# A spectral filter and a feed-forward layer on one core: the first batch in halves of d, one of them turned by DMA transposes

## The chip, the cores and the metric

The kernel runs on one core of a Trainium2 chip. Its engines are PE (TensorE, matmuls, with PEld for the loads of stationary operands), DVE (VectorE), ACT (ScalarE), POOL (GpSimd) and SP (SyncE, which here only issues DMAs). DMAs are issued on the queues of SP, ACT and POOL and are carried by 16 DMA engines. The metric is the device time of one execution in microseconds (us); lower is better. The kernel before took 740.85 us, the median of 3 runs (740.0 to 741.22).

## The reference

x is 8 batches x 3008 positions x 256 channels (d), all in float32. Each batch is filtered along its positions in the frequency domain, and each of the 24064 resulting rows goes through a feed-forward layer:

```python
X = np.fft.rfft(x, axis=1)
F = (filt_r + 1j * filt_i)[None, :, :]
y = np.fft.irfft(X * F, n=x.shape[1], axis=1).reshape(B * S, D)
h = y @ w_in                      # 256 -> 2048
g = np.maximum(0.01 * h, h)       # leaky ReLU
out = g @ w_out                   # 2048 -> 256
```

## The kernel before

**The filter.** The 3008 positions are taken as 94 x 32 (N1 x N2). The transform is done as two matmul stages: the first contracts over the 94, the second, with the twiddles in its constants (f2_sb), over the 32. The filter is applied as two elementwise products (with the transform and with its real and imaginary rows swapped, `i` = 0 and 1), and two inverse stages follow. A matmul contracts over the partition axis, so between stage one and two, and again between the two inverse stages, the data must be turned: what lay along the free axis must come to lie along the partitions. The end of the filter is yt, 256 channels in two tiles of 128 partitions (`dt` = 0, 1) by a ring of 6 x 512 positions, in fp16.

**The feed-forward part.** 47 chunks of 512 rows. For each, `moe1` (L520) makes 16 column blocks of h on PE (L528) and ScalarE applies the leaky ReLU (L531); the second product is plain for the first three chunks (`plain`, L689) and after that a seven-product scheme (`products`, L633) whose sums and differences VectorE forms. Chunk 0 needs positions 0 to 511 of batch 0, which come from the first two groups h = 0, 1 of 376 positions, in both dt.

**Batches 1 to 7** are worked on beside the feed-forward part. Their first turn is a DMA transpose on SP's queue (`t1_load`, L274, issued at L277), their second goes through DRAM (L341, L285). When each group is issued is set by a planner: `at(time, f)` puts work into a heap by time, in units of which a chunk has SL = 8; PLANS, REST, READ, MARGIN, AFTER and the other constants of L102 to L126 give the due times. Every engine works in the order in which the program issues.

**Batch 0** comes before anything else can start and is written out by hand, in the string FIRST (L482), as a list of steps that is issued in order before the planner begins:

- `xc`, `blank`: rounding the first x columns (loaded early in float32 on SP, L225) to fp16, and zeroing the spare partitions of x_sb;
- `warm n`: n filler matmuls (L384) into a bank that is not read;
- `s1p`, `s1e`: stage one for some columns n0 into a PSUM bank, and its eviction by ACT (A) or VectorE (D) into big[0];
- `t1 i`: the first turn, a quarter of it each, a VectorE transpose of 32x32 blocks (L399);
- `s2p hf c n i b`: stage two for half hf of d, n of the 24 frequencies from c on; `s2d`: the filter product by VectorE straight from PSUM; `s2a`, `s2m`: a copy by ScalarE, then the product by POOL (L416);
- `sap`, `sae`: the first inverse stage (L436) and its eviction (L439) into big[2];
- `t2 i`: the second turn, a quarter each, by VectorE (L445) into big[0];
- `sbp dt h b`, `sbe`: the last inverse stage (L453) and its eviction into yt (L351). What FIRST leaves out of it is done later by the planner (`late_sb`, L464, at the times REST);
- `x 0`, `x 1`, `w_out`: loads of batch 1's x and of w_out, on POOL's queue.

In the kernel before, `t1` and `t2` turn all 256 channels in four quarters, both halves of d go through the same buffers, and all eight groups h of dt 0 and two of dt 1 are in FIRST.

**Queues at the start.** SP: the first constants (L224), six columns of x in float32 (L225), the other constants (L226). POOL, in this order: the other x columns in three loads (L207), two thirds of f2_sb (L230), the filters of the first half of d (L215, four loads with rows of 256 bytes), the rest of f2_sb (L236), the filters of the second half, the constants of the last inverse stage (L237), w_in (L238, 2 MB in float32). POOL issues these between 1.24 and 18.2 us. Its products, and then batch 1's x in two halves and w_out, follow in its order. Of POOL's loads, each waits at its issue for the one eight before it to land.

**The tail.** `last_three` (L668) stores the last four tiles as they become ready: m4_tile the columns of two tiles (of which the second is cut in 120 and 8 rows), m3_tile those of the other two.

Of the kernel before, what the change touches and what calls it, by code (L numbers as in the profile page):

```python
# [11 lines left out]
P = 128  # L12
FP16 = mybir.dt.float16
FP32 = mybir.dt.float32
# [5 lines left out]
N1, N2 = 94, 32  # L20
# [58 lines left out]
def kernel(  # L79
# [26 lines left out]
    READ = 1.712  # L106
    TURN = 0.889
    TURNED = 2.3
    TURNS = 1.015
    MARGIN = 3.838  # L110
    YD = (0.966, 1.75, 0.753, 0.432, 1.2)
    SUMS_FIRST = (0.018, 2.103, 2.35, 4)
    SUMS = (0.322, 1.569, 2.418, 4)
    REST = (5.339, 14.69, 8.396, 11.015, 24.419, 20.72)
# [3 lines left out]
    AFTER = (0.454, 0.757, 1.245, 2.615, 0.39, 0.731)  # L118
# [3 lines left out]
        (0.01, 0.254, 12.6, 1.065, 4.3, 35.584, 2.78, 8.122, 1.518),  # L122
        (23.983, 0.737, 42.87, 2.58, 7.4, 85.174, 2.85, 2.756, 2.12),
# [98 lines left out]
    EARLY = 6  # L222
# [4 lines left out]
    for n0, nn in ((6, 10), (16, 10), (26, 6)):  # L227
        x_load(0, n0, nn)
# [9 lines left out]
    nc.gpsimd.dma_start(w_in_sb[:], moe_w_in.rearrange("(dt p) c -> p dt c", p=P))  # L238
# [6 lines left out]
    nc.vector.memset(big[2][:].rearrange("p (e n t) -> p e n t", n=Q, t=2)[:, :, NC:Q, :], 0.0)  # L245
# [44 lines left out]
    def paired(t):  # L290
        return t[:].rearrange("p (e n t) -> p n e t", n=Q, t=2)

    def spread(dst, n0, ps, copy, e0=0):
        nn, de = ps.shape[1], ps.shape[2] // 2
        copy(paired(dst)[:, ds(n0, nn), ds(e0, de)], ps.rearrange("p n (e t) -> p n e t", t=2))

    E4 = D // 2 // 4

    def first_t1(i):
        a = big[0][:].bitcast(FP32)[:, ts(i, E4 * Q)].rearrange("p (e n r) -> p e n r", n=Q // 2, r=2)  # L300
        o = big[1][:].bitcast(FP32).rearrange("p (n e r) -> p e n r", n=Q // 2, r=2)
        nc.vector.transpose(o[:, ts(i, E4)], a)
# [84 lines left out]
    def s1p(_, n0, n, b):  # L387
        ps = fill(("s1", n0), b, n, D)
        for j in range(0, n, 2):
            nc.tensor.matmul(ps[:, ds(j, 2), :], fwd1[:N1], x_sb[:N1, ds(n0 + j, 2), :],  # L390
                             start=True, stop=True)

    def s1e(_, n0, n, e):
        spread(big[0], n0, held.pop(("s1", n0)), engine[e])

    def t1(i):
        a = big[0][:].bitcast(FP32)[:, ts(i, E4 * Q)].rearrange("p (e n r) -> p e n r", n=Q // 2, r=2)
        o = big[1][:].bitcast(FP32).rearrange("p (n e r) -> p e n r", n=Q // 2, r=2)
        nc.vector.transpose(o[:, ts(i, E4)], a)  # L399
# [424 lines left out]
```

## Time and profile before

| what | value |
|---|---|
| median of 3 runs | 740.85 us (740.0 to 741.22) |
| the profiled execution | 740.64 us, its span 738.8 us |
| PE busy | 730.5 us, 99% of the span |
| DVE, ACT, POOL busy | 69%, 74%, 23% |
| chain that ended last | PE 93% |
| first feed-forward matmul (L528) | 34.71 us after the span's start |
| end of VectorE's last turn in FIRST | 33.74 us |
| x_sb, w_in, w_out loads from issue to landing (median) | 8.1, 13.1, 14.3 us (480 KB, 1024 KB, 1024 KB) |
| last DMA issue (ACT's queue) | 735.85 us, 0.57 us long |

The span runs from the first to the last instruction; the execution's own time has 1.8 us around it. In the page's table of slices each digit is the busy share of one of 40 slices (18.5 us each) in tenths. A DMA share above 1 means that several records are under way in one DMA engine. In a line of the timeline stand start, length, engine, line, operation, the tiles written and read, shapes, count, and in brackets the idle time before it with what ended it. The rows of L528 on PE give 0.21 us for a matmul of 512 columns in a row with others.

### The profile page before, as it was taken

How to read it: one execution, taken by the hardware profiler on the slowest of the kernel's cores; microseconds unless marked ns; L12 is line 12 of the kernel's file. 1: busy time of each engine (PE TensorE's matmuls, PEld its weight loads, DVE VectorE, ACT ScalarE, POOL GpSimd, SP SyncE). 2: the span in 40 equal slices, each digit the busy share in tenths (PEclk: the TensorE clock that was granted, in tenths of full speed). 3: DMA queues.
4: the chain of work that ended last, by engine and by line, in shares of the span. 5: the costliest groups of instructions: out<-in, count | busy, mean ns of one | idle time of the engine just before them, and what ended most of it. 6: DMA issues, size and time to landing. Idle time of an engine off the chain costs nothing.

```text
span 738.8 us, 19530 instructions
## 1 busy us (share of the span) xinstructions
PE 730.5 (99%) x8129; PEld 521.8 (71%) x8129; DVE 508.7 (69%) x696; ACT 549.3 (74%) x763; POOL 168.0 (23%) x171
## 2 busy tenths in 40 slices
PE   8999999999999999999999999999999999999997
PEld 3666677777777777777777777777767777777776
DVE  7878557776677667676777668666767676465566
ACT  4775787887788778887688777888767777777762
POOL 5605411333221312212132322222031220000000
PEclk9999999999999999999999999999999999999999
DMA  9978778778755595556855477434863433112012
GB/s 203 228 109 171 189 150 170 178 172 167 188 134 126 138 193 143 130 145 126 183 131 137 122 157 169 115 90 110 149 172 95 117 106 94 55 55 66 29 46 71
DMA packets 128617, 98.44 MB, mean 133 GB/s; under 512 B 59296, under 2 KB 107296, under 8 KB 128336
## 3 DMA queue, kind: packets, MB, share of 16 engines
q1 hardware_dynamic: 112905, 79.37, 42.0%
q0 software_dynamic: 15056, 17.50, 15.7%
q8 instruction: 63, 1.03, 0.6%
q10 hardware_dynamic: 567, 0.32, 0.2%
q14 instruction: 26, 0.21, 0.1%
HBM read 45.97 MB, written 35.65 MB: 110 GB/s over the span
## 4 chain that ended last, share of the span: by engine, by line
PE 93%; SPq 2%; DMA 2%; DVE 1%; ACT 1%; POOL 0%; issue 0%; POOLq 0%
PE ph L528 42%; PE pf L601 18%; PE po_ps L601 18%; PE pf L269 2%; PE pf L362 2%; PE pf L315 2%; PE pf L337 2%; PE pf L693 1%; DMA x_sb<-in_x_dram 1%; PE po_ps L693 1%; SPq L277 1%; SPq L587 1%; DMA p_b_g<-p_b_g 1%; PE po_ps L384 0%; PE pf L436 0%; ACT yt L351 0%
## 5 line engine op out<-in xcount | busy, mean ns | idle before, releaser
L531 ACT ACTIVATE gt_c<-ph 128x1024 f16<-128x1024 f32 x376 | 385.4, 1025 | 132.3 <-PE ph L528 125.5
L528 PE MATMUL ph<-yt,w_in_sb 128*128 128x512 f16 x1504 | 447.3, 379 | 0.2 <-ACT yt L351 0.2
L601 PEld LDWEIGHTS <-gt_c 128*128 128x128 f16 x2800 | 201.8, 98 | 97.9 <-issue 1.3
L330 POOL TENSOR_TENSOR y_b_g<-p_b_g,p_b_g 128x512 f16<-128x512 f32 x84 | 118.1, 1407 | 421.1 <-DMA p_b_g<-p_b_g 288.1
L601 PEld LDWEIGHTS <-big 128*128 128x128 f16 x2128 | 151.4, 98 | 65.9
L528 PEld LDWEIGHTS <-w_in_sb 128*128 128x128 f16 x1504 | 117.7, 98 | 4.4 <-DVE yt L351 0.4
L324 DVE TENSOR_TENSOR p_b_g<-pf,fb_sb 128x512 f32<-128x512 f32 x78 | 53.7, 688 | 33.8 <-PE pf L315 20.3
L601 PE MATMUL po_ps<-wt_sb,gt_c 128*128 128x128 f16 x704 | 71.8, 219 | 0.0
L601 PE MATMUL pf<-wt_sb,gt_c 128*128 128x128 f16 x688 | 69.3, 219 | 0.0
L601 PE MATMUL pf<-wt_sb,big 128*128 128x128 f16 x704 | 68.7, 219 | 0.0
L601 PE MATMUL pf<-w_out_sb,gt_c 128*128 128x128 f16 x720 | 68.1, 219 | 0.0
L351 ACT CAST yt<-pf 128x376 f16<-128x376 f32 (+9 forms) x136 | 58.1, 441 | 12.2 <-PE pf L362 8.5
L601 PE MATMUL po_ps<-w_out_sb,gt_c 128*128 128x128 f16 x688 | 65.7, 219 | 0.0
L601 PE MATMUL po_ps<-wt_sb,big 128*128 128x128 f16 x688 | 65.5, 219 | 0.0
L567 DVE TENSOR_TENSOR gt_c<-gt_c 128x2048 f16<-128x2048 f16 x43 | 56.9, 1322 | 1.0
L327 DVE TENSOR_TENSOR p_b_g<-pf,fa_sb 128x512 f32<-128x512 f32 x84 | 57.2, 681 | 0.2
L567 DVE TENSOR_TENSOR big<-gt_c,big 128x2048 f16<-128x2048 f16 (+1 forms) x45 | 56.4, 1254 | 0.0
L567 DVE TENSOR_TENSOR big<-big,gt_c 128x2048 f16<-128x2048 f16 (+1 forms) x45 | 56.3, 1252 | 0.1
L567 DVE TENSOR_TENSOR big<-gt_c 128x2048 f16<-128x2048 f16 (+1 forms) x46 | 56.3, 1224 | 0.0
L339 ACT CAST big<-pf 128x512 f16<-128x512 f32 x84 | 49.0, 584 | 9.3 <-PE pf L337 7.4
L270 ACT CAST big<-pf 128x384 f16<-128x384 f32 x90 | 43.0, 479 | 11.5 <-PE pf L269 8.2
L362 PE MATMUL pf<-i_sb,big 128*128 128x94 f16 x448 | 37.0, 206 | 0.0
(98 smaller groups left out, 644.7 us busy)
## 6 DMA issues: line engine op xcount, KB each, us to landing
p_b_g<-p_b_g SPq DMA_DIRECT2D x156, 128.0 KB
out_dram<-ost_c_h SPq DMA_DIRECT2D x118, 128.0 KB
dz<-big SPq DMA_DIRECT2D x42, 256.0 KB
big<-dz SPq DMA_DIRECT2D x56, 192.0 KB
x_sb<-in_x_dram POOLq DMA_DIRECT2D x40, 192.0 KB, 4.2
x_sb<-in_x_dram POOLq DMA_DIRECT2D x2, 768.0 KB, 9.2
w_in_sb<-in_moe_w_in_dram POOLq DMA_DIRECT2D x1, 1024.0 KB, 13.1
w_out_sb<-in_moe_w_out_dram POOLq DMA_DIRECT2D x1, 1024.0 KB, 14.3
```

Source lines behind the costliest of these rows:

```text
L269: nc.tensor.matmul(ps[:, j, :], x_sb[:, 4 * h + j, ts(dt, P)], fwd1m[:, :NW], start=True, stop=True)
L270: copy(turn_in[:, :, dt, :, ds(4 * h, 4)], ps.rearrange("p n (q k) -> p k q n", q=4))
L324: nc.vector.tensor_tensor(p2[:], ps, fb, AL.mult)
L327: nc.vector.tensor_tensor(p1[:], ps, fa, AL.mult)
L330: ("y", b, g), lambda: nc.gpsimd.tensor_tensor(y1[:], p1[:], p3[:], AL.add)))
L339: nc.scalar.copy(st2[h % 3][:, ds(2 * (g % 2), 2), :], ps)
L351: copy(yt[:, dt, ds(to, 4 * n)].rearrange("p (a c) -> p a c", c=4), v[:, ds(a, n)])
L362: nc.tensor.matmul(ps[:, j, :], z2[h % 3][:, j, ts(dt, P)], i1_sb[:, 4 * h + j, :N1], start=True, stop=True)
L528: nc.tensor.matmul(ph[:, j, :], w_in_sb[:, dt, ts(ct, P)], yt[:, dt, ds(ci * CH % RING, CH)], start=(dt == 0), stop=(dt == NDT - 1))
L531: nc.scalar.activation(gts[ci][:, ds(2 * g, 2), :], ph, AF.Lrelu)
L567: nc.vector.tensor_tensor(*(v[:, ds(c0, n)] for v in (o, i0, i1)), op)
L601: nc.tensor.matmul(of[t], a()[:, c, ts(t, P)], w[:, c, :], start=(c == 0), stop=(c == NCH - 1))
```

## The change

- d is split: half 0 (channels 0 to 127) is turned by VectorE before stage two, now in two quarters (`t1`), half 1 by three DMA transposes of eight frequencies each on SP's queue (`turn1`). For that, stage one of half 1 is computed with x as the stationary operand, 96 columns at a time, so that channels lie on the partitions.
- Before the last inverse stage it is the other way round: half 0 is turned by four DMA transposes of eight columns each (`turn2`), half 1 by VectorE in two quarters (`t2`). Half 0's first inverse stage now has the product as the stationary operand: 48 matmuls of 128 columns in place of 12 of 512.
- The steps of FIRST stand in another order; VectorE evicts three of the groups of `sae`. `sbp` in FIRST covers h = 0 to 3 of dt 0 (and 0, 1 of dt 1); h = 4 to 7 of dt 0 are done later, at the times REST0.
- w_in comes in two pieces, as steps of FIRST on POOL's queue; `x 0` is issued ahead of POOL's first product, the second piece of w_in among the products.
- The early x load has eight columns, the other three loads eight each.
- At the end, m4_tile's first store goes to ACT's queue and its second to SP's, and both of m3_tile's to ACT's.
- Constants of the planner have other values.

```diff
-    READ = 1.712
+    READ = 1.863
...
-    REST = (5.339, 14.69, 8.396, 11.015, 24.419, 20.72)
+    REST = (5.723, 13.479, 13.889, 13.394, 25.953, 17.309)
+    REST0 = (0.946, 2.627, 7.4, 12.566)
...
-    EARLY = 6
+    EARLY = 8
...
-    for n0, nn in ((6, 10), (16, 10), (26, 6)):
+    for n0, nn in ((8, 8), (16, 8), (24, 8)):
...
-    nc.gpsimd.dma_start(w_in_sb[:], moe_w_in.rearrange("(dt p) c -> p dt c", p=P))
...
+    half = [t[:, ts(i, HALF)] for t in big for i in range(2)]
+    in0, in1, mid0, mid1, in2, in3 = half
...
+    def s1p(t, n0, b):
+        if t == 0:
+            ps = fill(("s1", t, n0), b, 4, DH)
+            nc.tensor.matmul(ps, fwd1[:N1], x_sb[:N1, ds(n0, 4), :DH], start=True, stop=True)
+            return
+        ps = fill(("s1", t, n0), b, 4, NW)
+        for j in range(4):
+            nc.tensor.matmul(ps[:, j, :], x_sb[:N1, n0 + j, DH:], fwd1m[:N1, :NW], start=True, stop=True)
...
+    def turn1(c, n):
+        nc.sync.dma_start_transpose(mid1[:, ds(c, n)], in1[:, ds(c, n)].rearrange("p k q n -> p (k q n)"))
+
+    def turn2(h, n):
+        nc.sync.dma_start_transpose(out2[:, ds(h, n)], in2q[:, ds(h, n)].rearrange("p n q k -> p (n q k)"))
...
+    def load_w_in(i):
+        half = moe_w_in.shape[1] // 2
+        nc.gpsimd.dma_start(w_in_sb[:, :, ts(i, half)], moe_w_in.rearrange("(dt p) c -> p dt c", p=P)[:, :, ts(i, half)])
...
     def sap(hf, c, b):
         ps = fill(("sa", hf, c), b, 4, DH)
+        if hf == 0:
+            for j in range(4):
+                for i, m in enumerate((inv2r, inv2i)):
+                    nc.tensor.matmul(ps[:, j, :], prods[0][:, i, c + j, :], m, start=(i == 0), stop=(i == 1))
+            return
...
+            if dt == 0:
+                nc.tensor.matmul(ps[:, j, :], out2[:, n2], i1_sb[:, n2, :N1], start=True, stop=True)
+                continue
...
     FIRST = """
+        blank 2, warm 14, blank 3, s1p 0 8 b2, blank 0, xc 4 4 D, blank 1, s1p 0 4 b4, xc 0 4 A, s1p 0 0 b3,
+        s1p 1 0 b0, s1e 0 4 A, s1p 1 4 b1, s1e 1 0 D, s1e 0 0 A, s1e 1 4 A, s1p 0 20 b4, s1p 1 8 b0, s1e 1 8 A,
+        s1p 0 12 b3, s1e 0 8 D, s1p 1 12 b1, s1p 0 16 b0, s1e 0 12 D, s1e 1 12 A, s1p 1 20 b1, s1p 0 28 b3,
+        w_in 0, s1e 0 16 A, s1p 0 24 b2, s1e 1 20 A, s1e 0 24 A, s1e 0 20 D, s1e 0 28 D, t1 1, s1p 1 16 b1,
+        s1p 1 24 b4, s1p 1 28 b2, warm 6, s1e 1 16 A, t1 0, s2p 0 0 8 0 b3, s1e 1 24 A, s1e 1 28 A,
+        s2p 0 0 8 1 b4, turn1 16 8, turn1 0 8, s2p 0 16 4 1 b1, s2p 0 16 4 0 b0, s2a 0 16 4 0, s2d 0 0 8 0,
+        s2a 0 16 4 1, s2p 0 8 8 0 b3, x 0, s2p 0 20 4 0 b2, s2d 0 0 8 1, s2p 0 20 4 1 b0, s2d 0 8 8 0,
+        s2a 0 20 4 0, s2p 0 8 8 1 b4, s2m 0 16 4 0, s2a 0 20 4 1, sap 0 0 b1, sap 0 4 b2, s2p 1 16 4 0 b0,
+        sae 0 0 A, s2d 0 8 8 1, s2p 1 0 8 0 b3, sap 0 8 b1, sae 0 4 A, s2p 1 0 8 1 b4, s2m 0 20 4 0,
+        s2a 1 16 4 0, s2d 1 0 8 0, turn1 8 8, s2p 1 16 4 1 b0, s2d 1 0 8 1, sae 0 8 A, s2m 0 16 4 1,
+        sap 0 12 b2, sap 0 16 b1, s2m 1 16 4 0, s2a 1 16 4 1, s2m 0 20 4 1, sae 0 12 A, s2p 1 8 8 0 b3,
+        sap 0 20 b2, sae 0 16 D, w_in 1, sae 0 20 A, s2d 1 8 8 0, s2p 1 20 4 0 b0, s2m 1 16 4 1, s2p 1 8 8 1 b4,
+        s2a 1 20 4 0, s2p 1 20 4 1 b1, sap 1 0 b2, s2d 1 8 8 1, sap 1 16 b3, sae 1 0 A, sap 1 4 b0, turn2 0 8,
+        sae 1 4 A, turn2 8 8, sap 1 12 b4, turn2 16 8, sap 1 8 b2, s2m 1 20 4 0, s2d 1 20 4 1, x 1, sae 1 12 A,
+        sae 1 16 D, sap 1 20 b1, turn2 24 8, sbp 0 0 b3, sae 1 8 D, sae 1 20 A, t2 1, sbe 0 0 A, warm 2, t2 0,
+        w_out, sbp 0 1 b3, sbe 0 1 D, sbp 0 2 b0, sbe 0 2 D, sbp 0 3 b2, sbp 1 0 b4, sbp 1 1 b1, sbe 0 3 A,
+        sbe 1 0 D, sbe 1 1 A
     """
...
-            soon(0.02, lambda: (nc.sync, nc.scalar)[t].dma_start(*parts[0]))
+            soon(0.02, lambda: (nc.scalar, nc.sync)[t].dma_start(*parts[0]))
...
-            soon(0.02, lambda: store(ci, 2 + t, low[:, t, 1], P, P, queue=(nc.sync, nc.scalar)[t]))
+            soon(0.02, lambda: store(ci, 2 + t, low[:, t, 1], P, P, queue=nc.scalar))
...
+    for h in range(4, 8):
+        at(REST0[h - 4], lambda h=h: late_sb(0, h, act))
```

## The prediction

> **What bounds the kernel now.** First the page's table of slices, for the engine that is full and for the state of the DMA engines.
>
> ```profile
> PE   8999999999999999999999999999999999999997
> DMA  9978778778755595556855477434863433112012
> ```
>
> PE is full from the second slice to the last but one; the DMA engines are fullest in the first two, 0 to 37 us. So I split PE's time at the first matmul of the feed-forward part (answer on stretches: stretch, length, then busy time and count of PE, PEld, DVE, ACT, POOL, clock, DMA share, GB/s).
>
> ```profile
> 0.00:34.70 34.70, 31.70 (x309) 16.70 (x310) 29.76 (x34) 20.55 (x36) 21.92 (x31) 1.00 1.18 217
> 34.70:46.40 11.70, 11.62 (x112) 6.79 (x112) 8.90 (x15) 9.84 (x14) 1.33 (x2) 1.00 0.97 151
> 46.40:735.16 688.76, 687.19 (x7710) 498.35 (x7709) 470.07 (x648) 518.87 (x715) 144.71 (x138) 1.00 0.55 129
> ```
>
> After 34.7 PE works through a fixed list without a hole worth naming; the change can move the start of that list (T0 = 34.71), its content, or the tail. What sets T0, by the chain in order of time and the timeline:
>
> ```profile
> 2.43 9.88 DMA x_sb<-in_x_dram
> ...
> 27.90 1.22 DVE prod L416
> 29.11 2.29 DVE big L445 x2
> ...
> 31.93 2.74 ACT yt L351 x7
> 34.67 0.04 issue
> 34.71 0.38 PE ph L528
> ```
>
> ```profile
> 14.23 4.62 DVE L399 STREAM_TRANSPOSE big<-big 128x1024 f32<-128x1024 f32 x4
> ...
> 18.40 4.51 POOL L416 TENSOR_TENSOR prod<-spare,fa_sb 128x512 f16<-128x512 f32 x4 [0.25 <-DMA fa_sb<-in_filt_i_dram]
> ...
> 23.42 2.30 POOL L416 TENSOR_TENSOR prod<-spare,fa_sb 128x512 f16<-128x512 f32 x2 [0.50 <-DMA fa_sb<-in_filt_i_dram]
> ...
> 29.03 4.71 DVE L445 STREAM_TRANSPOSE big<-big 128x1024 f32<-128x1024 f32 x4
> ```
>
> The reader is to see two clocks: VectorE (turn, filter products, turn; the last turn ends at 33.74, T0 0.97 later), and POOL's loads, whose filters arrive at 18.3 (first half of d) and 23.3 (second).
>
> What the change adds exists already from batch 1 on, as L277, and its company is on record:
>
> ```profile
> L277 SPq DMA_TRANSPOSE big<-big x42: 1247/1330/2988, 49.0 to 532.9; - x42
> ```
>
> ```profile
> 176.38 1.40 SPq L277 DMA_TRANSPOSE big<-big  x1
> ```
>
> ```profile
> 176.43 0.54 POOL L207 DMA_DIRECT2D x_sb<-in_x_dram  x1
> ```
>
> I counted the trace's packet records. A turn of 128x1024 is 1024 records of 256 B; undisturbed, first records come 1.2 us after issue, all 16 engines are taken for 1.3 us, and it lands 3.2 us after issue (48.96 to 52.14); turns in a row follow 1.3 us apart. The one issued at 176.38 met the load of 176.43 (2048 B records): from 178.6 to 179.4 the load passed 47 records and the turn 41; once the load was out the turn ran at 200 per 0.2 us, and ended at 181.5, 2 us late. Over all 112 steps of 0.2 us after 46 us with both queues busy, POOL's queue passed 1533 records and SP's 1266, whatever their sizes. Likewise the second constants load (128 KB, SP, issued 1.66) landed at 9.9, among the x loads. So the rings take turns record by record, and a 256 B record pays for a large one each time.
>
> **The change, part by part.**
>
> *Removed from VectorE:* two of four turns at each end, 2 x 1.155 = 2.3 us and 2 x 1.18 = 2.35 us. *Added:* three evictions (0.66 each, 2.0 us) and one quarter product (0.68) taken from POOL. The first gain is lost: the last x lands at 12.31 as before (same bytes), the two remaining turns end between 16.4 and 17.2 (ScalarE evicts 0.66 + 0.47 + 0.47 + 0.66 per step before them), but the products need the first filters, at 18.3.
>
> *First turns (3 on SP, issued 15.6 to 16.3):* they run beside the filters' 256 B records. Each needs 1.28 us of all engines, 3.8 us in all; this pushes POOL's ring back by 3.8 us if times add, by 0 if they overlap (the filters' DMA share of 1.8 means two records in flight per engine). I take 1.9: second filters at 25.3. VectorE then runs 25.3 + 2 x 1.22 + 0.66 + 2 x 1.22 + 0.68 + 2 x 0.66 + 2 x 1.18 = 35.2; with 1.0 for the last matmuls and evictions T0 cannot be before 36.2 (34.3 to 38.1).
>
> *Second turns (4 on SP):* they wait for all six evictions of the first half. POOL's order puts a second-half product first, so 25.3 + 2 x 1.16 + 0.6 (two matmuls) + 0.66 = 28.9, first records 30.2 (28.6 to 32). What is in POOL's ring then is the point. Before: constants to 24.1, w_in to 28.6, two halves of x to 36.3, w_out to 41.6, without a gap. After: constants, half w_in, x, half w_in, x, w_out; same bytes, since nothing on POOL waits for a turn. w_in passes 52 records a us, x 25, w_out (512 B) 385. By the end of the second x, 36.3 + 1.9 + 0.3 = 38.5, the first turn has passed at most some 270 records of 1024. Beside w_out the pair makes 263 a us if times add and 385 if they overlap, I take 310: the other 750 take 2.4 us, the second turn 3.3, with 0.5 to land 44.7 (41.7 to 47.7). PE's order needs this second turn ahead of the second half's last matmuls: four groups, evictions, 2.0 us (0.97 for two before). T0 = 46.7 (43.7 to 49.7): +12.0 us (9.0 to 15.0). Turns three and four land by then or soon after; their matmuls come 1.9 us after T0 or later.
>
> [...]
>
> *Cold PE:* PE has little after 31 until the first second turn lands. The row nearest is its only other idle time, before the first fillers: their weight loads come 0.42 us apart up to 5.44, then seven in 1.41. Half speed for 4.2 us costs 2.1 if it happens again and 0 if not; I take 2.0, for that row. [...]
>
> *Work moved behind T0:* four groups of four 94-column matmuls, at 0.17 (the like groups of L269 in the chain): +0.7 us, as PE is full there. Their four evictions (0.47) fit in ScalarE's 1.9 us idle of 11.7.
>
> *POOL and SP queue:* the first x load (0.6 to issue) goes ahead of the products, the w_in half (0.7) among them; POOL's first three products still end by 22.5, ahead of the filters at 25.3, and the rest is earlier than the turns. SP has nothing else to issue before 46. The constants load that now feeds the fourth first-stage step lands up to 0.9 later, 10.7; last x at 12.3 and the filters at 18.3 cover it. First-stage matmuls (16 of 512 columns become 8, and 32 of 96) and the 48 small inverse ones lie under those waits; smaller blanking too.
>
> *Tail:*
>
> ```profile
> 734.30 1.45 ACTq L677 DMA_DIRECT2D out_dram<-ost_c_h  x1
> 735.85 0.57 ACTq L587 DMA_DIRECT2D out_dram<-ost_c_h  x1
> ```
>
> The last store waits 0.7 us behind a 120-row one. Swapped, ACT is free at 735.3, but SP has the 120-row store (1.0 to 1.45) and an 8-row one (0.70): the last issue ends 736.05 to 736.45 against 736.42. I take -0.2 (-0.4 to 0).
>
> *Retuned times* move work inside a stretch where PE is full: 0; the two idle spots of PE there sum to about 2 us (1.2 at one wait for POOL near 536, some 0.7 at 34.7 to 46.4), so -1 to +1.
>
> Sum, against the profiled execution's 740.64: +12.0 + 2.0 + 0.7 - 0.2 = 755.1; the median of the runs is 0.2 above that execution, so 755.3.
>
> **The rivals.**
>
> [...]
>
> 2. *Faster.* VectorE's chain is shorter by 4.65 - 2.68 = 2.0 us. If filters and turns never hold it, T0 = 32.7 and the time is 740.64 - 2.0 + 0.7 - 0.2 - 0.7 (the holes behind T0) = 738.4. It decides only if the first filters are there at 17.2, not 18.3, the second by 23, and the second turns land by 31.5. Against: POOL's ring was full from 2 to 43 us.
>
> 3. *No change.* Turns hidden, filters at 18.3 and 23.3 as now: VectorE ends at 33.3, T0 34.3: 740.64 - 0.4 + 0.7 - 0.2 = 740.7.
>
> **How the numbers follow.** Starved turns 0.74, own range 749 to 762 (749.8 = +9.0, no cold PE; 759 = +15.0 and cold, with 1 us for the holes, and more if the turns overlap badly); rival 1 0.12, rival 2 0.07, rival 3 0.07. Two in ten to be left out: the range takes in most of rival 1, 742 to 762. A difference of 0.2% (1.5 us) is about what a measurement of this kernel can tell from none. Faster: rival 2, 0.07. Same: rival 3 and a little of rival 1, 0.09. Slower: 0.84.
>
> **What the profile after would show.** Right: PE waits of several us before L453 for the second turns, first feed-forward matmul at 44 to 50 and not 34.7, first turns' waits of 1 to 3 us more than 3.2, the second filters later than 23.3, weight loads 0.42 apart behind the wait, PE's list from T0 on about 700 us as now. [...] What would break it most is a POOL ring that runs empty around 27 to 33, because w_in's second half or x is issued later than I read from POOL's order.

## The result and the profile after

The changed kernel took 783.74 us, the median of 5 runs (781.45 to 786.58); before took 740.85 (5 runs beside it, 740.0 to 741.57): a ratio of 1.058, with an interval of 1.0548 to 1.0613. The prediction was 755.3 us with a range of 742 to 762: slower, as forecast, but by 42.9 us and not by 14.5. The profiled execution is the fastest of the five, 781.45 us, its span 779.7; the figures below account for it, and not for the 2.3 us between it and the median.

First the page's table of slices after the change (each digit the busy share of one of 40 slices of 19.5 us, PEclk the granted clock in tenths), and the chain by lines:

```profile
PE   7237999999999999999999999999999999999997
PEclk7658999999999999999999999999999999999999
DMA  9999577778696559555685549534574432212112
GB/s 204 147 56 169 93 148 180 158 172 182 151 184 156 134 129 189 142 136 145 126 184 131 128 112 166 166 95 114 105 178 124 112 105 82 83 49 68 35 42 69
PE 87%; DMA 8%; SPq 2%; POOL 1%; DVE 1%; ACT 0%; issue 0%; POOLq 0%; DVEq 0%
PE ph L555 40%; PE pf L628 17%; PE po_ps L628 17%; DMA big<-big 6%; PE pf L362 2%; PE pf L337 2%; PE pf L278 2%; PE pf L315 2%; DMA p_b_g<-p_b_g 1%; PE po_ps L720 1%; PE pf L720 1%; DMA x_sb<-in_x_dram 1%; POOL y_b_g L330 1%; SPq L286 1%; PE pf L454 0%
```

PE is now full only from the fifth slice on, where before it was from the second. The telling slice is the third, 39 to 58 us: its DMA digit is 9, and it moved 56 GB/s. The engines of the DMAs were busy and passed almost nothing. The turns (big<-big) are 6% of the chain, 45 us by its pieces below. The same by stretches of the changed kernel, and last the second stretch in the kernel before (length, then busy time and count of PE, PEld, DVE, ACT, POOL, clock, DMA share, GB/s):

```profile
0.00:24.00 24.00, 18.77 (x148) 10.42 (x148) 16.19 (x21) 10.91 (x20) 13.80 (x24) 0.79 1.26 200
24.00:51.00 27.00, 0.61 (x4) 0.34 (x4) 0.00 (x0) 0.58 (x1) 3.67 (x4) 0.53 1.27 95
51.00:58.00 7.00, 6.62 (x96) 6.15 (x98) 3.96 (x4) 2.44 (x5) 1.14 (x1) 0.63 0.69 84
58.00:69.06 11.06, 5.61 (x59) 3.06 (x53) 6.89 (x10) 3.60 (x7) 2.86 (x3) 0.88 1.00 155
69.06:73.20 4.14, 3.91 (x22) 1.91 (x21) 1.46 (x3) 1.91 (x3) 0.54 (x1) 0.50 1.35 183
73.20:775.00 701.80, 698.12 (x7819) 504.82 (x7817) 480.68 (x659) 529.00 (x729) 144.05 (x139) 1.00 0.55 128
```

```profile
24.00:51.00 27.00, 26.35 (x290) 16.26 (x287) 22.28 (x30) 21.49 (x36) 7.55 (x9) 1.00 0.87 158
```

From 24 to 51 us hardly an engine works (PE 0.61 us of 27), and 95 GB/s pass at a DMA share of 1.27; before, the same 27 us moved 158 GB/s at a share of 0.87. After 73.2 PE is full again. The chain in order of time says for what the engines waited:

```profile
16.12 1.36 SPq L409
17.53 33.81 DMA big<-big
...
58.40 0.76 SPq L412
59.20 1.33 SPq L412
60.58 11.35 DMA big<-big
71.97 0.49 PE pf L477 x4
```

and the timeline, on SP and on PE:

```profile
16.12 27.84 SPq L409 DMA_TRANSPOSE big<-big  x3
57.93 4.60 SPq L412 DMA_TRANSPOSE big<-big  x3
```

```profile
67.54 0.81 PE L477 MATMUL pf<-i_sb,big 128*128 128x94 f16 x8 [5.10 <-DMA big<-big]
...
69.06 1.22 PE L555 MATMUL ph<-yt,w_in_sb 128*128 128x512 f16 x2
```

The second of the three first turns, issued at 17.53, landed at 51.3; even to issue three of them took SP 27.84 us. T0 is 69.06 (46.7 was forecast, 34.71 is before's). The sum over the trace closes: T0 +34.35, from T0 to the last matmul 705.81 for 699.91 (+5.9), from there to the span's end 4.79 for 4.21 (+0.6), together 40.8 over before's span of 738.8.

Landings by the semaphores, with what was forecast: first turns 29.4, 51.3, 56.1; second filters 38.2 (25.3); w_in's first half 46.6; x's first half 50.1; second turns issued at 57.9 to 62.6 (28.9) and landed at 61.2, 67.5, 71.9, 76.6. I counted packet records: from 21 to 23.5 us the filters and the turns passed one for one, some 330 a us each; then, with the first 6144-byte records of i1 (the constants of the last inverse stage), the turns' 256-byte records began to last up to 2.4 us (18 ns alone), i1's up to 3.9 (0.24 in the kernel before). Of SP's 2840 records from 20 to 52 us, 631 lasted over 0.15 us. Both streams were held, where the prediction had only the turns wait.

### The profile page after: what moved, and what is told of

It is laid out like the page before. It is cut to its first block, busy times and chain, and to the rows that moved or that the text cites. A ratio compares the mean times of both kernels' runs of the same rounds, so it can differ in the third digit from the quotient of the medians.

```text
span 779.7 us, 19560 instructions
## 1 busy us (share of the span) xinstructions
PE 733.7 (94%) x8134; PEld 526.7 (68%) x8134; DVE 509.5 (65%) x696; ACT 548.4 (70%) x764; POOL 166.1 (21%) x171
## 4 chain that ended last, share of the span: by engine, by line
PE 87%; DMA 8%; SPq 2%; POOL 1%; DVE 1%; ACT 0%; issue 0%; POOLq 0%; DVEq 0%
PE ph L555 40%; PE pf L628 17%; PE po_ps L628 17%; DMA big<-big 6%; PE pf L362 2%; PE pf L337 2%; PE pf L278 2%; PE pf L315 2%; DMA p_b_g<-p_b_g 1%; PE po_ps L720 1%; PE pf L720 1%; DMA x_sb<-in_x_dram 1%; POOL y_b_g L330 1%; SPq L286 1%; PE pf L454 0%
## 5 line engine op out<-in xcount | busy, mean ns | idle before, releaser
L324 DVE TENSOR_TENSOR p_b_g<-pf,fb_sb 128x512 f32<-128x512 f32 x78 | 53.6, 687 | 34.0 <-PE pf L315 21.7
L351 ACT CAST yt<-pf 128x376 f16<-128x376 f32 (+7 forms) x137 | 58.8, 442 | 19.4 <-PE pf L362 9.6
L594 DVE TENSOR_TENSOR big<-gt_c 128x2048 f16<-128x2048 f16 (+1 forms) x46 | 58.9, 1281 | 0.2 <-ACT gt_c L558 0.2
L279 ACT CAST big<-pf 128x384 f16<-128x384 f32 x92 | 44.1, 480 | 12.9 <-PE pf L278 11.1
```

The source lines that it names most:

```text
L279: copy(turn_in[:, :, dt, :, ds(4 * h, 4)], ps.rearrange("p n (q k) -> p k q n", q=4))
L324: nc.vector.tensor_tensor(p2[:], ps, fb, AL.mult)
L351: copy(yt[:, dt, ds(to, 4 * n)].rearrange("p (a c) -> p a c", c=4), v[:, ds(a, n)])
L594: nc.vector.tensor_tensor(*(v[:, ds(c0, n)] for v in (o, i0, i1)), op)
```

## The experiments

Theories: A, the rings of SP and POOL pass record for record and each record takes its own time (the prediction's); B, a large record beside a turn takes many times its own time; C, a backlog of several turns does it; D, in a DMA transpose the 16 DMA engines keep step, and one that is ahead holds its engine, for both queues, until the others come up; D2, D with the order of record sizes that drives the engines apart. Times are of one execution, beside 739.9 to 741.7 of before, where no interval is given.

**Turns and loads alone.** A kernel of its own with turns and loads.

> A kernel that computes nothing of the reference and writes only 128 rows of the output: ten stages, each begun when the one before has landed: three turns of 128x1024 alone; three loads like the constants of the last inverse stage (6144 B records, 128 each) alone, then beside three turns; three x loads (8192 B records) alone, then beside three turns; three small x loads (2048 B) beside three turns; four w_in pieces beside three turns; filter loads (256 B) beside three turns; filters, constants, w_in and x in a row beside three turns; the constants beside one turn. Theory A, the rings alternate record by record and each record takes its own time: three turns alone take 6 us from the first issue to the last landing, three constants loads 6 to 8 us, both together 10 to 12 us; x loads 12 to 14 us, with turns 15 to 18; no stage over 20 us. Theory B, records of several kB beside a turn take many times their own time: the stages with 6144 and 8192 B records take over 25 us with three turns, that with 256 B records 10 to 12 us as under A. Theory C, it is the backlog of several turns: over 25 us with three turns beside any load, but the last stage, with one turn, under 10 us.

The loads began only when the turns had landed, so nothing overlapped. It gives the times alone: a turn lands 3.1 to 3.4 us after its issue, turns in a row are issued some 1.3 us apart, and the 128 records of 6144 bytes of one load begin within 2.8 us.

**Three turns added to before.**

```diff
+    for i in range(3):
+        nc.sync.dma_start_transpose(wt_sb[:, i], f2_sb[:, ts(2, NC // FP), :].rearrange("p k m -> p (k m)"))
```

> The kernel before, with three DMA transposes of 128x1024 added on SP's queue behind the landing of the last third of the second stage's constants (19.2 us); nothing reads what they write before it is overwritten. Theory A: 1500 turn records pass beside filters, constants, w_in and x, POOL's loads come 1.5 to 2.5 us later, first feed-forward matmul at 35 to 37, time 741 to 743. Theory B: constants and w_in are held up as in the changed kernel, 10 us or more; first feed-forward matmul at 45 or later, time 751 or more. Theory C says as B. If the trouble were in how the changed kernel's own steps wait for one another, this kernel would lose nothing: 740 to 741.

767.7 us, 27 more, for three turns that nothing reads. T0 nearly stays (35.84); then PE waits 21.7 us for x:

```profile
PE pf L271 <- DMA x_sb<-in_x_dram: 21.7, 1, 21.7
```

Beside w_in's 4096-byte records (24 to 29 us) both queues passed 48 records a us, one for one and near w_in's own rate (52 in the kernel before), as by A; groups of one number of records on both sides would give the same counts. With the change from w_in to x, at 30 us, both queues nearly stopped, up to 62 (51 GB/s from 30 to 38 us).

**Turns and loads apart.** In the changed kernel POOL issues i1, w_in's first half and x's first half only after the first turns have landed (`hold 1`); then also w_in's second half, x and w_out only after the first two second turns (`hold 2`).

```diff
-    nc.gpsimd.dma_start(i1_sb[:], i1_d.ap())
...
+    def hold(of):
+        t = mid1 if of == 1 else out2
+        nc.gpsimd.tensor_copy(mark[:, 0:1], t[:, 7, 0:1])
+        nc.gpsimd.tensor_copy(mark[:, 1:2], t[:, 15, 0:1])
...
+        ... s2m 0 20 4 1, hold 1, i1, w_in 0, x 0, sae 0 12 A, ...
```

> The changed kernel, but POOL issues the last inverse stage's constants, the first half of w_in and the first half of batch 1's x only after all three first turns have landed (it reads an element of two of them first). The first turns then meet filters alone: all theories have them landed by 28 us, not 56. The second turns still meet w_in and x. Theory A, the prediction's sum for them: first feed-forward matmul at 44 to 52, time 749 to 762. Theory B: the second turns clog as the first did; first feed-forward matmul over 55, time over 763.

> As the run with the first hold, and also the second half of w_in, batch 1's x and w_out are issued only after the first two second turns have landed; so neither set of turns has loads of large records beside it but the end of the constants and the first half of w_in. All theories that blame the loads: first feed-forward matmul at 35 to 41; batch 1's x then comes 5 to 9 us after it and PE waits for it; time 743 to 752. If the turns are slow by themselves in this place, the first feed-forward matmul stays over 50 and the time over 757.

769.22 and 762.75 us. With the first hold the first turns landed at 26.3, 27.7 and 28.5, and the second ones ran as the prediction's rule has it: issued at 33.67 and 35.09 they landed at 51.7 and 56.0, while w_in, x, w_in and x beside them landed some 3 to 4 us apart (39.1, 42.5, 45.4, 49.2), none of them stopped, and w_out at 57.7, in 8.6 us for 5.3 in the kernel before. The waits of PE (line waited for: us in total, times, longest):

```profile
PE ph L486 <- DMA big<-big: 15.0, 1, 15.0
PE pf L421 <- DMA big<-big: 3.1, 1, 3.1
```

So a turn beside large records starves and the loads don't stop: the trace has A's mechanism, though T0 (57.59) and time lie where B was to have them. The expectation had left out that the hold itself puts off the loads, i1 from 16.9 to 29.9 us, and that the turns starve beside them for as much longer. With both holds the second turns land 3 to 6 us after issue and T0 is 41.8, but then PE waits 8.7 us for x, and the time is 11 us over the expected 743 to 752: from T0 to the last matmul it takes 14.5 us more than before, of which the 8.7 are the largest part. Moving the loads away gets T0 and gives it back.

**Loads that run when the turns come.**

> This kernel computes nothing of the reference; it only moves data, in ten stages that wait for each other, and writes 128 rows. In each stage the loads of POOL's queue start first and SP's DMA transposes (128x1024, fp16) come while they run: (1) three turns alone, (2) four loads of constants with 6144-byte records alone, (3) these beside three turns, (4) four x loads with 8192-byte runs alone, (5) these beside three turns, (6) these beside one turn, (7) eight pieces of w_in with 4096-byte records beside three turns, (8) eight filter loads with 512-byte rows beside three turns, (9) two filters, constants, x beside three turns, (10) filter, constants, a piece of w_in and x beside three turns. Theory A (rings alternate record by record and each record takes its own time): no stage takes longer than its loads alone plus 1.3 us a turn, so at most 4 us more; the turns land up to as late as the loads. Theory B (a record of some kilobytes beside a turn takes many times its own time): stages 3, 5 and 7, and 9 and 10, take 15 to 30 us more than their loads alone, stage 8 nothing; stage 6 some third of it. Theory C (only several turns waiting at once do it): stage 6 is as by A, stages 3, 5 and 7 as by B. If no stage stalls, it needs something else than loads and turns together, and the size of records alone is ruled out.

Four x loads took 17.2 us alone, 17.9 beside three turns, 17.8 beside one; four constants 10.4 and 11.3; the turns were starved to the end of them. B falls. Only the last two stages, with small records before large ones, were held, by some 4 us: in the one the last filter load ended on the DMA engines from 162.1 to 166.2, in the other w_in (2048-byte records, before x's 8192) took 6.9 us after the load before it, where a piece takes 2.9.

**One turn at a time, and plain copies.** The three added turns write one tile, so that each waits for the one before; or they are plain copies of the same 256-byte pieces.

```diff
-        nc.sync.dma_start_transpose(wt_sb[:, i], f2_sb[:, ts(2, NC // FP), :].rearrange("p k m -> p (k m)"))
+        nc.sync.dma_start_transpose(wt_sb[:, 0], f2_sb[:, ts(2, NC // FP), :].rearrange("p k m -> p (k m)"))
```

> The kernel before with three DMA transposes at the start that nothing reads, all to one destination, so that each is issued only when the one before it has landed: one turn is under way at any time. With all three issued in a row it took 767.7 us, 27 more than before. Theory C (a backlog of several turns makes the stall): the loads get back most of it, 741 to 750 us, and each turn costs x at most some microseconds. Theory B (any turn beside large records): 755 to 770 us, with x landing at 50 or later. Theory A alone (record by record, each in its own time): 741 to 745 us, since the loads then lose at most 3.8 us.

```diff
+    spread_to = wt_sb[:].rearrange("p i c d -> p (i c d)").rearrange("p (k m) -> p k m", k=NC // FP)
-        nc.sync.dma_start_transpose(wt_sb[:, i], f2_sb[:, ts(2, NC // FP), :].rearrange("p k m -> p (k m)"))
+        nc.sync.dma_start(spread_to[:, :, ts(i, P)], f2_sb[:, ts(2, NC // FP), :])
```

> The kernel before with three plain copies in SBUF at the start that nothing reads, of the same 128x1024 fp16 in the same 256-byte pieces and in the same place on SP's queue as the three DMA transposes that took 767.7 us. If it is the transpose that makes the stall: 740 to 746 us, x landing at 35 to 42 as the ring of the loads is pushed back by no more than the copies' own time (3 x 1.3 us). If any small records on another queue beside the loads of POOL do it: 760 to 770 us, x landing after 50.

751.37 and 741.86 us, beside 739.95 of before. The stretch from 30 to 38 us, first with one transpose at a time, then with copies:

```profile
30.00:38.00 8.00, 5.08 (x89) 3.31 (x87) 4.93 (x6) 4.65 (x12) 0.48 (x1) 0.99 1.83 46
```

```profile
30.00:38.00 8.00, 7.42 (x117) 5.00 (x116) 6.88 (x9) 6.15 (x13) 1.22 (x2) 1.00 1.04 205
```

46 GB/s against 205: it takes a transpose, and one is enough to start a stop, so C falls as its cause; but 751.37 lies between the ranges of C and B, and one turn at a time (the second was issued at 44.6, when x's first half had landed) costs 11 us and three in a row 27. With copies x landed at 34.6 (34.4 before), and of 3120 records on SP none lasted over 76 ns. With the one transpose 201 of 1056 lasted over 150 ns. The 4-byte records at its end show how (26 of them): they began at 34.48, 35.10, 35.74, 36.35, 36.99 and 37.60, 0.62 us apart, which is the time of one x record (0.625), and most lasted from 0.6 up to 6.6 us. Read by theory D, the engines that were ahead waited while another, behind them, passed large record after large record.

**The tail alone.**

```diff
-            soon(0.02, lambda: (nc.sync, nc.scalar)[t].dma_start(*parts[0]))
+            soon(0.02, lambda: (nc.scalar, nc.sync)[t].dma_start(*parts[0]))
...
-            soon(0.02, lambda: store(ci, 2 + t, low[:, t, 1], P, P, queue=(nc.sync, nc.scalar)[t]))
+            soon(0.02, lambda: store(ci, 2 + t, low[:, t, 1], P, P, queue=nc.scalar))
```

> The kernel before with only the tail of the change: the first store of the last four tiles on ACT's queue, the second on SP's, and both of the other pair's on ACT's. By the prediction's step the last issue ends 0 to 0.4 us earlier: 740.65 us, ratio 0.9995 to 1. By the rival read from the trace of the changed kernel, where the last issue ended 0.1 us sooner after VectorE's last addition but the span ended 3.09 us after that issue and not 2.40: 741.2 us, 0.3 to 0.6 us more, too little for the median to tell and to be read from the span behind the last matmul (4.21 us before).

Ratio 0.9999 (0.9989 to 1.0009). From the last matmul to the span's end 4.08 us for 4.21.

**The planner's constants alone.**

```diff
-    READ = 1.712
+    READ = 1.863
...
-    REST = (5.339, 14.69, 8.396, 11.015, 24.419, 20.72)
+    REST = (5.723, 13.479, 13.889, 13.394, 25.953, 17.309)
```

> The kernel before with only the planner's constants of the change (READ, TURNS, MARGIN, YD, SUMS, REST, AFTER, PLANS). The prediction put them at 0, from -1 to +1: 740 to 742 us, ratio 0.999 to 1.001. The changed kernel took 5.9 us more than before from the first feed-forward matmul to the last, of which a cold PE (2.1 us, at half clock from 69.06 to 73.19) and the four late groups (0.7) explain 2.8: if the constants make the other 3.1, this takes 743 to 744 us, ratio 1.003 to 1.005.

742.33 us, ratio 1.0018 (1.0005 to 1.0031), that is 1.3 us (0.4 to 2.3). In its profile T0 to the last matmul takes 701.8 us, 1.9 more than before.

**Turns of the changed kernel as plain copies.** All seven; the three first; the four second ones.

```diff
-        nc.sync.dma_start_transpose(mid1[:, ds(c, n)], in1[:, ds(c, n)].rearrange("p k q n -> p (k q n)"))
+        nc.sync.dma_start(mid1[:, ds(c, n)], in1[:, ds(c, n)].rearrange("p k q n -> p k (q n)"))
...
-        nc.sync.dma_start_transpose(out2[:, ds(h, n)], in2q[:, ds(h, n)].rearrange("p n q k -> p (n q k)"))
+        nc.sync.dma_start(out2[:, ds(h, n)], in2q[:, ds(h, n)].rearrange("p n q k -> p n (q k)"))
```

> The changed kernel with each of its seven DMA transposes of the first batch replaced by a plain copy of the same bytes in the same 256-byte pieces, on the same queue, in the same place (the copies don't turn, so the first batch's result is not the reference's; all other work and all waits are as they were). If the transposes themselves made both streams stop from 24 to 51 us, what is left is the prediction's mechanism, copies passed over record by record: T0 at 44 to 50, 750 to 760 us. If small records on SP's queue beside POOL's loads are enough, 775 to 785 us and T0 near 69.

> The changed kernel with the three first turns alone replaced by plain copies (which don't turn, so half of the first batch's result is not the reference's); the four second turns stay DMA transposes. By the prediction's step for the second turns (starved one record for one, loads at their own rate) T0 is 44 to 50 and the time 750 to 760 us, as with all seven replaced. If the second turns make the loads stop as well where w_in, x and w_out run in sequence beside them: T0 55 to 70, 762 to 785 us.

> The changed kernel with the four second turns alone replaced by plain copies (which don't turn, so half of the first batch's result is not the reference's); the three first turns stay DMA transposes. The changed kernel took 783.74 us, with the first turns as copies 782.95, with all seven as copies 754.19. If each of the two groups makes the loads stop by itself: last first turn at 50 to 57, T0 at 60 to 68, 772 to 782 us. If the first turns' stop was worth nothing (what the second turns cost they cost in any case): 754 to 762 us.

754.19, 782.95 and 780.13 us; T0 42.98, 69.79, 67.59. Either group of transposes stops the loads by itself: with the second as copies the first turns land at 30.7, 53.3 and 59.1; with the first as copies, which land by 24.3, the four second turns bring the stop, and x's second half lands at 68.0. That 754.19 lies so near the forecast is chance. The expectation was wrong on the copies: source and destination were contiguous, and the records were of 2048 bytes, 128 a copy, so they were passed over far less. So once more, each copy split in two of every second block, which keeps pieces of 256 bytes (at twice the DMAs on SP's queue):

```diff
+        for a in range(2):
+            nc.sync.dma_start(mid1[:, ds(c, n)].rearrange("p (k a) m -> p a k m", a=2)[:, a],
+                              in1[:, ds(c, n)].rearrange("p (k a) q n -> p a k (q n)", a=2)[:, a])
```

> The changed kernel with each of its seven DMA transposes replaced by two plain copies of every second block, so that the pieces stay 256 bytes (in the run with seven plain copies whole rows were joined to records of 2048 bytes, 128 a copy; there T0 was 42.98 and the time 754.19). The copies don't turn, so the first batch's result is not the reference's. By the prediction's step for small records passed over one for one: second turns starved beside w_in and x, T0 44 to 50, 750 to 760 us. If small records in that number are enough to stop both queues, transposes or not: T0 over 55, 765 us and more.

769.01 us, T0 58.79. These are the numbers of the second case, but not its cause: no record on SP lasted over 82 ns, and the loads didn't stop. The last filter landed at 27.5 (23.3 before), and from there i1, w_in and x's first half took 11.4 us (11.1 before). But the first turns landed only at 39.5. PE's waits for the turns, before stage two (L426) and before the last inverse stage (L481):

```profile
PE ph L426 <- DMA big<-big: 10.7, 2, 6.7
PE pf L481 <- DMA big<-big: 7.7, 3, 6.3
PE pf L426 <- DMA big<-big: 2.7, 1, 2.7
```

With records passed one for one and nothing held, the change costs 27 us beside the 741.70 of before; with transposes 43.

**What drives the engines apart.** Three kernels that only move data. A load of 20 rows lies on 10 of the 16 DMA engines, two rows on each (six of its 16 updates come 1.5 us after the issue, the ten others at 3.3 us and more, as read in the second of the three), so the others get ahead. The first expectation has its rows spread otherwise, which was wrong.

> Computes nothing of the reference: nine stages that wait for each other, in each some loads on POOL's queue and, while they run, DMA transposes or plain copies of 128x1024 on SP's. Three x loads (96 records of 8192 bytes each, six for each DMA engine) stand alone (stage 1), with two turns (2); behind four small x loads of 20 rows, which give four engines one record more each than the others, so that they fall behind by some 2.5 us (3 alone, 4 with two turns, 5 with two plain copies); behind four x loads of 4 rows (6 alone, 7 with one turn, 8 with one copy); and four loads of constants behind the 20 rows, with two turns (9). Theory D (a turn's records on the 16 engines keep step: an engine that is ahead waits in its turn record for the engine that is behind, and what the loads have on that engine waits too): stages 4, 7 and 9 have turn records of 0.3 us and more, in multiples of the x record's time, and their loads land at least 4 us later than in 3 and 6; stages 5 and 8 have none, with loads at most 2 us later; stage 2 as stage 1 with at most 2 us more. Theory A (record by record, each in its own time): no stage's loads land more than 2 us later for its turns, and no turn record takes over 0.15 us. If 4, 7 and 9 are as 3 and 6, engines out of step are not enough, and what else the kernels bring (engines at work on SBUF, loads of several sizes) stays open.

The small loads wrote one tile and waited for each other, so most turns fell between loads. Two pairs did meet. In one, a turn beside a single load of 20 rows landed 7.95 us after issue and not 3.2, the load 7.4 and not 3.7 to 3.9, with x records of up to 3.9 us; in the other, in the last stage, they took 5.2 and 4.6.

> Computes nothing of the reference: eight stages that wait for each other, each with six loads on POOL's queue, all into tiles of their own: four small ones of x rows of 8192 bytes, then two of 96 such rows. In stages 1 to 4 the small ones have 20 rows (these lie on 10 of the 16 DMA engines, two on each, so that the other six come 5 us sooner to the large loads), in 5 to 7 32 rows (two on every engine); stage 8 has two loads of constants (6144 bytes, 128 rows) in their place. Beside them come, some microseconds later, on SP: nothing (1, 5), one DMA transpose (2), two (3, 6, 8), two plain copies in the same 256-byte pieces (4, 7). Theory D (in a turn the engines keep step; one that is ahead waits in its turn record for one that is behind, and holds the loads' records on it): the last load lands in 2 and 3 at least 4 us later than in 1, with turn records of 0.3 us and more; in 4, 6, 7 and 8 at most 2.6 us later than in 1 or 5, with no turn or copy record over 0.15 us but at the ends. If a change of record size is enough without engines out of step: 8 stalls too. Theory A (each record in its own time): no stage is more than 2.6 us later than its loads alone.

With tiles of their own: 15.9 and 16.1 us from the first issue to the landing of the last load with one and with two turns, 16.1 with copies; with 32 rows, by the same count two on each of the 16, 15.1 alone, 15.6 with two turns, 16.6 with copies; the last stage took 15.1. Engines out of step alone cost no more time than copies do, though D's mark is there: beside one turn, 197 of its records passed from 59 to 60 us (at most some 33 on each of the six engines ahead), and then the next ones took up to 1.26 us, two x records long, and ended together at 60.6, 61.2, 61.8 and 62.3; and the last x load ended on all engines within 0.2 us (2.9 with copies). The stage without turns had its issues 2.1 us apart and can't be compared.

> Computes nothing of the reference: eight stages that wait for each other. Loads on POOL's queue: two small x loads of 20 rows (these lie on 10 of the 16 DMA engines, which fall 2.5 us behind the other six), six filter loads (256-byte records on all engines) and two x loads (8192-byte records). Stage 1: the 20 rows and three turns. Stage 2: 20 rows, filters, x, alone; 3: the same with three DMA transposes on SP; 4: with three plain copies in the same 256-byte pieces. Stage 5: 20 rows, x, filters, alone; 6: with three turns. Stage 7: filters, x, alone; 8: with three turns. Theory D2 (the engines keep step in a turn; an engine that is behind in the loads and still in the small records passes more turn records than one that is already in the large ones, so it is held and falls further behind, until both queues nearly stop): 3 takes at least 8 us more than 2, with turn records of 0.6 us and more and engines that end a load over 5 us apart; 4 at most 3.9 us more than 2; 6 at most 3.9 us more than 5 (the engine that is behind is in the large records there, and is slow in both queues); 8 up to 3.9 us more than 7 if the engines stay in step, else as 3. If order and record size make no difference: 3 and 6 alike.

The stretches of the stages from first issue to last landing (length, busy DVE and POOL, clock, DMA share, GB/s); in order: small then large, alone, with turns, with copies; large then small, alone, with turns; small then large with all engines level, alone, with turns:

```profile
38.38:57.60 19.22, 5.26 (x12) 6.27 (x10) 1.00 1.13 161
59.14:104.20 45.06, 4.17 (x4) 6.29 (x10) 1.00 1.37 84
108.02:131.30 23.28, 4.62 (x8) 6.26 (x10) 1.00 1.12 166
134.29:154.00 19.71, 6.02 (x17) 6.27 (x10) 1.00 1.13 156
154.66:179.80 25.14, 5.89 (x16) 6.28 (x10) 1.00 1.14 154
180.61:200.30 19.69, 5.26 (x12) 5.24 (x8) 1.00 1.02 140
201.79:238.50 36.71, 4.01 (x3) 5.27 (x8) 1.00 1.32 86
```

Here is the stop of the changed kernel, with nothing but loads and turns: 256-byte records before 8192-byte ones take 25.8 us more beside turns and 4.1 beside copies, and the other order 5.4. The last filter load ended on the first DMA engine at 71.7 and on the last at 97.0. Engines that begin level, but for the 0.6 to 4.0 us by which some trail at the end of a filter load without turns too, stop as well: 17.0 us. Of the 3072 turn records, 579 and 413 lasted over 0.3 us in the two stages that stop, and 1 in the one with the large records first. So the stages come out as D2 has them, but for the 5.4, where it had at most 3.9; with one record held, they aren't a stop.

**x in small records.** The kernel before with the three turns, x in 512-byte records.

```diff
-        x_load(1, half * N2 // 2, N2 // 2)
+        n0 = half * N2 // 2
+        for a in range(2):
+            rows = x_sb[:R1, ds(n0, N2 // 2), :].rearrange("p (b a) d -> p a b d", a=2)[:, a]
+            nc.gpsimd.dma_start(rows, bass.AP(tensor=x.tensor, offset=x.offset + (N + n0 + a) * D,
+                                              ap=[[N2 * D, R1], [2 * D, N2 // 4], [1, D]]))
```

> The kernel before with the three DMA transposes that nothing reads (767.7 us), and with batch 1's x loaded in 512-byte records (every second row, in four loads) and not in 8192-byte ones (two loads). Theory D2: from w_in (4096 bytes) on to x the records now get smaller, an engine that is behind is slow in both queues, and nothing is held for long: x lands at 37 to 45, as turns and x pass one for one at about 235 a us each, and the time is 742 to 750 us. If any three turns beside these loads stop both queues whatever the records: 760 to 770 us.

754.88 us, between the two: half of the 27 us come back. x landed at 42.8 to 50.0, the three turns by 46.5, and 147 of SP's records (of 3168) still lasted over 0.15 us. Less of a stop, but a stop, where D2 had none; what part of the rest is holding and what is x's own sharing with the turns was not told apart.

## Why the prediction was wrong

**The step that failed** is "First turns (3 on SP, issued 15.6 to 16.3): they run beside the filters' 256 B records", with "I take 1.9". The chain holds 33.8 us of waiting for them. Four things were wrong in it.

- *Its price.* Where nothing was held (both runs with holds, and the first turns as copies) the second filters landed at 27.0 to 27.5, 3.7 to 4.2 us later than before's 23.3, and not 1.9: the times add.
- *When they run.* Beside the loads a turn's first record came 4.5 us after its issue (16.12 to 20.58), not 1.2; the seven-copies runs have 4.2 and 4.9, the added turns 4.1 to 4.4; why isn't shown. So the turns met the filters for some 3 us only, and then i1, w_in and x.
- *The prediction's own rule was not applied to them.* It let records pass one for one, and worked that out for the second turns alone. Of the first turns' 3072 records 1017 had passed by 24 us, when the filters were nearly out; the rest lay beside i1, w_in and x. With 256-byte copies, which do nothing but that, T0 is 58.79 and the time 769.0: 12.1 of the 22.4 us that T0 was forecast too early, with twice as many DMAs on SP's queue there.
- *A turn holds the loads.* No case of the prediction had it. The overlaps that it counted in the kernel before were short, and it counted how many records passed, not how long each lasted. The trace of before has the holding already, in the very turn of 176.38: behind the stretch that was counted, 19 of its 256-byte records begin from 179.69 to 180.05 us and all end from 180.27 to 180.31. At 52.84 to 53.11 another 19 begin and last up to 1.8 us, to 54.6, while the last 1024-byte records of a store on the same queue pass; in all, 208 such records behind 46 us last over 0.3 us. By D2, a DMA engine that is behind in the loads is still in the filters' 256-byte records, passes more turn records than one already in i1, gets ahead in the turn, is held, and falls further behind in the loads. The stages with small records before large ones show that this order makes the stop; that it does so by this chain of steps is argued, since which engine waited for which isn't in the traces, whose packet records don't name the engine. Transposes for 256-byte copies are the other 10.3 us of T0, and 783.7 for 769.0 in time.

**The second turns:** right in kind. Beside w_out (68 to 74 us) they were passed one for one, 240 records a us each; 263 was the lower end of the prediction. With the first turns out of the way (`hold 1`) the second of them landed 6.9 us after x's second half (56.0 and 49.2), where the prediction had 6.2 (44.7 and 38.5), and T0 came 1.6 us later (2.0). In the changed kernel they came so late that the second had passed nearly all its records before x's first one, at 61.9 us; the few that were left waited beside x until 67.5.

**T0 sets the end:** right. 34.35 of 40.8 us are T0.

**Cold PE, +2.0:** the clock row has 0.50 from 69.06 to 73.20, so 2.07 lost, and the weight loads there come 0.43 apart. The row has 0.50 from 67.50 on already, behind 5.5 us (62.0 to 67.5) of which PE was busy for 0.33; and in the 27 us from 24 to 51, with 0.61 us busy, the granted clock was 0.53.

**The list after T0,** forecast +2.7, is +5.9: 2.07 cold, 0.7 for the four late groups (not measured by itself), some 1.9 for the constants, put at 0 with 1 at most, and 1.3 more of waiting for POOL's y_b_g (2.7 us in three waits for 1.4 in two with the constants alone). **The tail,** -0.2: -0.1 in the profile alone, no difference in the median; the 0.6 more in the changed kernel is in no run explained.

**Rival 1** (0.12, and the low end of the range) has turns that pass several records for each large one of the loads. No run shows that: they passed 48 to 48 beside 4096-byte records (the three turns added to before), 240 to 240 beside 512-byte ones (the changed kernel). **Rivals 2 and 3** needed turns that nothing delays.

**Two figures of the prediction** don't come out of its rows. The low end 749.8 is 750.1 by its own terms. And where it has 1533 to 1266 records in 112 steps, the trace has, behind 46 us, 266 steps of 0.2 us with data records on both queues, 2174 of POOL's and 5888 of SP's. The rule of one for one rests on the row of 176.38 (47 to 41) and on the runs above.

No version beat before: with turns and loads kept apart T0 was at best 41.8, and x was late.

## What to carry to other kernels

A price that is used for one group of DMAs (here, small records are passed over one for one by large ones, 48 to 48 beside w_in) is to be applied to every group that shares the rings, with the time at which its records really start (here 4.5 us after the issue, and not 1.2). A DMA transpose is not a copy: beside loads on another queue whose records change from small to large, three of them made 45.06 us of 19.22, and three copies 23.28. Beside loads of one record size the transposes alone waited (four x loads took 17.9 us for 17.2), and with no loads each landed 3.1 to 3.4 us after its issue; so put transposes where that queue is empty or runs records of one size, and look for a stretch with a high DMA share and few GB/s (here 1.27 and 95, for 0.87 and 158 before). Read how long the records of an overlap last, and not only how many pass: the holding stood in the trace of before. When a replacement is to keep the record size, count the records: here adjacent pieces of 256 bytes were joined to 2048.

## What the runs showed of the hardware

- The 256-byte records of a DMA transpose last 18 ns alone and up to 2.4 us beside loads (a 4-byte one 6.6 us), and those that are held end together (19 of before from 180.27 to 180.31 us); 256-byte records of plain copies stay under 0.1 us (76 and 82 ns at most in two kernels). That a transpose keeps the DMA engines in step is the author's reading of these records. Three transposes beside loads of small records and then large ones cost 25.8 us of 45.06. How many records an engine may be ahead was seen once, at most some 33.
- On SP's queue the first record of a DMA comes 1.2 us after its issue when the rings are quiet, 2.1 after it beside the one x load at 176.43 of before, and 4.1 to 4.9 among the loads of the start.
- What starts the stop in the kernel before with added turns, where w_in's 4096-byte records go over to x's, is only argued from the above.
